# Linear attention into a Fourier mixing layer: even folds of the last two batches ahead of the odd ones, and the output stored through two disjoint views

## The chip, the cores and the metric

The kernel runs on one core of a Trainium2 chip. A core has a tensor engine (PE, whose weight loads are shown as PEld), a vector engine (DVE), a scalar engine (ACT), GpSimd (POOL) and a sync engine (SP) that issues transfers. Each engine takes its own instructions strictly in the order in which they were written for it, and engines wait for one another through semaphores. Transfers between the large memory (HBM) and the on-chip memory are started by SP, ACT or POOL. The metric is the device time of one execution in microseconds (us), lower is better. The time before is the median of three runs.

## The reference

Four batches of 768 positions go through two layers. The first is attention with a decay (8 heads of 64), in blocks of 64 positions, with a running state; its output becomes `x` of shape 4 x 768 x 512. The second is a Fourier mixing layer with a two-layer network:

```python
X = np.fft.fft(x, axis=1)
X = np.fft.fft(X, axis=2)
mixed = np.real(X)
u = x + mixed
un = (u - mean(u)) / np.sqrt(var(u) + 1e-06)
ch = np.maximum(un @ w_ch1, 0.0) @ w_ch2
return u + ch
```

`w_ch1` is 512 x 2048 and `w_ch2` is 2048 x 512. Everything is in 32-bit floats.

## The kernel before

**Stages.** The attention of a batch is computed in six chunks of 128 positions (`attn_in`, `attn_out`). The two-dimensional Fourier transform's real part is computed with cosine and sine matrices, after the input has been folded: positions and features that share a cosine (or, up to sign, a sine) are added or subtracted first, so that the matrices become smaller. Then come the normalization and the network. The network of the first four groups of rows (`PLAIN`, two row tiles of 128 each) is computed directly in `mlp`; the other eight groups (`LATE`) are put away in HBM and computed afterwards in four pairs with Strassen-like products, seven instead of eight (`first_layer`, `deep_first`, `deep_second`).

**Folds.** For each of a batch's two row blocks (`BLK`, 128 and 65 rows), `fold_a` makes the first half of the folds as soon as most of the attention is there, and `fold_b` the second half, when the last gathered rows have landed (the gather is an indirect transfer of POOL, line 461). `fold_b` goes through block 0 and then block 1. In each it makes an even operand `fe` (additions, lines 435, 438, 479, 480, 484, 485, with one small ACT copy on line 475) and an odd operand `fo` (subtractions, lines 436, 439, 488, 489, 492, 493). All of them run on DVE, and the built order alternates even and odd steps. Lines 435 and 436 are wide (512 elements per row), the others narrow (about 256).

**Products along the positions.** `fft_ln`, lines 520 to 530, makes five products `i` from these operands. Products 0, 1 and 4 read only `fe`, products 2 and 3 only `fo`. Each consists of four matmuls (line 525): two halves `n`, and in each block 0 and then block 1. An ACT copy (line 529) brings each result to the on-chip memory as `ys`, which the products of `width` (lines 537 to 542) read. The products are made in the order 0, 1, 2, 3, 4.

**What PE does beside it.** The folds of batches 2 and 3 are interleaved with the network of the plain groups: lines 643 (first layer), 649 and 651 (relu, on DVE and ACT in turn), 657 (second layer), 668 and 669 (DVE adds the residual to `y`). The interleaving is decided at build time from the amounts that the generators yield, so that a changed `yield` or a changed order of the folds also moves instructions of the network between them. The same holds for SP's queue.

**The end.** The last layer of the last pair is made by `deep_second(j, k)` for k = 0 to 6. Products k and k + 1 are interleaved: each consists of seven steps of four matmuls (`mm`, line 1047), and after each step `read` adds a quarter of the result on DVE (line 1055) or copies it on ACT (line 1053). `seven` fixes the order of the seven steps and which quarter each reads. The last product, k = 6, makes the second half of the columns of two row tiles, `yt[:, 0, 0]` and `yt[:, 0, 1]`. In the given order, the quarters of tile `yt[:, 0, 0]` end at steps 1 and 6, those of tile `yt[:, 0, 1]` at steps 4 and 5.

**Stores.** `store` (lines 628 to 634) writes a finished row tile. The first three row tiles of a batch lie in order and are stored by SP. The others are mirrored rows in reverse order, which an indirect store on POOL scatters row by row to the output. An indirect store gives the whole output as its destination, so the dependence tracking orders each direct store after the indirect stores recorded before it, and the other way round: SP waits until the rows have landed. At the end of a pair, `deep_second` issues four stores: after k = 5 the indirect one of `yt[:, 1, 1]`, after k = 6 the indirect one of `yt[:, 0, 1]` and the direct ones of `yt[:, 1, 0]` and `yt[:, 0, 0]`.

Of the kernel before, what the change touches and what calls it, by code (L numbers as in the profile page):

```python
# [9 lines left out]

# [6 lines left out]
ALU = mybir.AluOpType  # L17
# [59 lines left out]
def kernel(  # L77
# [10 lines left out]
    nc = tc.nc  # L88
    B, H, S, D = q.shape
    DM = H * D  # L90
# [3 lines left out]
    HC = NC // 2  # L94
# [4 lines left out]
    HM = DM // 2  # L99
    QM = DM // 4  # L100
    W = HM + 4
    BLK = [128, S // 4 + 1 - 128]
# [36 lines left out]
    def new(pool, shape, tag, **kw):  # L139
        cnt[0] += 1  # L140
        return pool.tile(shape, F32, tag=tag, name=f"{tag}{cnt[0]}", **kw)

    def psum_a(shape):
        return new(pa, shape, "pa")
# [40 lines left out]
    def row_of(j, n=128):  # L185
        return bass.IndirectOffsetOnAxis(ap=ix[0:n, j:j + 1], axis=0)
# [56 lines left out]
    xs, xn_, xd = {}, {}, {}  # L243
# [12 lines left out]
    ins, oTs, eo = {}, {}, {}  # L256
# [173 lines left out]
    def fold_x(b, a, n, i, lo, hi):  # L430

        e, o = eo[b][a]
        tt = nc.vector.tensor_tensor

        tc.keep_in_program_order(tt(e[0:n, i, 0:DM], lo, hi, op=ALU.add))
        tc.keep_in_program_order(tt(o[0:n, i, 0:DM], lo, hi, op=ALU.subtract))
        yield 1.4
        tt(e[0:n, i, 1:HM], e[0:n, i, 1:HM], e[0:n, i, HM:DM - 1], op=ALU.add)
        tt(o[0:n, i, 1:HM], o[0:n, i, 1:HM], o[0:n, i, HM:DM - 1], op=ALU.subtract)
        yield 0.8  # L440
# [24 lines left out]
    def fold_a(b):  # L465
        for a, n in enumerate(BLK):
            yield from fold_x(b, a, n, 1, eo[b][a][1][0:n, 1, 0:DM], xn_[b, HC + a][0:n])

    def fold_b(b, sets):

        tt = nc.vector.tensor_tensor
        for a, n in enumerate(BLK):
            yield from fold_x(b, a, n, 0, xs[b, a][0:n], xs[b, HC + a][0:n])
            e, o = eo[b][a]
            nc.scalar.copy(e[0:n, :, HM:HM + 1], e[0:n, :, DM - 1:DM])

            am, bm = e[0:n, :, W:2 * W], o[0:n, :, W:2 * W]
            lo, hi = e[0:n, 0, 0:HM + 1], e[0:n, 1, 0:HM + 1]
            tt(am[:, 0, 0:HM + 1], lo, hi, op=ALU.add)
            tt(am[:, 1, 0:HM + 1], lo, hi, op=ALU.subtract)  # L480
            yield 0.8

            lo, hi = am[:, :, 0:QM], am[:, :, HM:QM:-1]
            tt(e[0:n, :, 0:QM], lo, hi, op=ALU.add)
            tt(e[0:n, :, QM:HM], lo, hi, op=ALU.subtract)
            yield 0.8
            lo, hi = o[0:n, 0, 1:HM], o[0:n, 1, 1:HM]
            tt(bm[:, 0, 1:HM], lo, hi, op=ALU.subtract)
            tt(bm[:, 1, 1:HM], lo, hi, op=ALU.add)
            yield 0.8  # L490
            lo, hi = bm[:, :, 1:QM + 1], bm[:, :, HM - 1:QM - 1:-1]
            tt(o[0:n, :, 0:QM], lo, hi, op=ALU.subtract)
            tt(o[0:n, :, QM:HM], lo, hi, op=ALU.add)
            yield 0.8
            sets.append((e, o))
        eo.pop(b)
# [3 lines left out]
    def fft_ln(b):  # L500
        sets = []

        def piece(a, i, n):

            c0 = W + QM if i == 4 else QM * (i % 2)
            return sets[a][i in (2, 3)][0:BLK[a], n, c0:c0 + QM]

        if b in LEADS:
            yield from fold_a(b)
            yield from fold_b(b, sets)  # L510
            yield 2.0
        else:
            yield 1.0
            run(fold_a(b))
            yield 6.0 if b - 1 in LEADS else 3.0
            run(fold_b(b, sets))
            yield 12.0 if b - 1 in LEADS else 9.0


        for i in range(5):  # L520
            ps = psum_a([128, 2, NK])
            m = 128 if i < 4 else 1
            for n in range(2):
                for a, rows in enumerate(BLK):
                    mm = nc.tensor.matmul(ps[:, n, :], lhsT=piece(a, i, n), rhs=cs[0:rows, a, i in (2, 3), n, :],  # L525
                                          start=(a == 0), stop=(a == 1))
                    if i + n + a == 0:
                        tc.keep_in_program_order(mm)
            nc.scalar.copy(ys[i][0:m, 0:2 * NK].rearrange("p (k n) -> p n k", n=2), ps[0:m])
            yield 1.4  # L530
# [66 lines left out]
        for t in (1, 2, 0):  # L597
            ps = psum_a([128, DM])
# [13 lines left out]
            if t == 0:  # L612
                ps = psum_a([128, DM])
# [11 lines left out]
    ORDER = [(b, g) for b in range(B) for g in (1, 2, 0)]  # L625
    PLAIN, LATE = ORDER[:4], ORDER[4:]

    def store(b, T, y, cols=slice(0, DM)):
        if T < HC:
            nc.sync.dma_start(out[b, 128 * T:128 * T + 128, cols], y[:, cols])  # L630
        else:
            nc.gpsimd.indirect_dma_start(out=out.rearrange("b s d -> (b s) d"),  # L632
                                         out_offset=row_of(2 + HC * (b + 1) + T - HC),
                                         in_=y[:, :], in_offset=None)

# [75 lines left out]
    def quarters_a(t):  # L711

        return [t[:, s, i:i + HF // 2] for s in range(2) for i in (0, HF // 2)]

    def quarters_b(t):

        return [t[:, i:i + HF // 2, m:m + HM // 2] for i in (0, HF // 2) for m in (0, HM // 2)]
# [44 lines left out]
    def bank():  # L762
        return new(s2.ps, [128, DM], "p2")
# [12 lines left out]
    PAIRS = len(LATE) // 2  # L776
# [171 lines left out]
        for s in range(G):  # L948
            e.tensor_tensor(o[:, s], x[:, s], y[:, s], op=op)

    def seven(mm, read):

        X, Y, Z = (bank() for _ in range(3))
        for m, ps, start, where in ((0, X, True, (0, 0, 1)), (1, Y, True, (0, 0, 0)), (2, X, False, (1, 0, 1)),
                                    (3, Z, True, (1, 1, 1)), (4, X, False, (1, 1, 0)), (5, Z, False, (1, 0, 0)),
                                    (6, X, False, (0, 1, 1))):
            if m:
                yield 0.0
            mm(m, ps, start)
            read(ps, *where)  # L960
# [70 lines left out]
    def deep_second(j, k):  # L1031

        P = pairs[j]
        h, (a, b) = P.h, PRODUCTS[k]
        y11, y12, y21, y22 = P.y
        if k == 0:
            P.t = new(s2.yp, [128, G, HM], "t2")
        T = P.t
        y, fresh = ((T, 1), (y11, 1), (y22, 1), (T, 0), (y12, 1), (y21, 0), (y12, 0))[k]
        A11, A12, A3, A22 = [[t[:, i] for i in range(HF // 2)] for t in quarters_a(h[a])]  # L1040
        B11, T3, B21, B22 = quarters_b(s2.B[b])
        (S1, S2, S4), (T1, T2, T4) = P.pre_a.pop(k), P.pre_b.pop(k)
        ab = [(A11, B11), (A12, B21), (S2, T2), (A3, T3), (S1, T1), (A22, T4), (S4, B22)]

        def mm(m, ps, start):
            for i in range(HF // 2):
                nc.tensor.matmul(ps[:, 0:HM // 2], lhsT=ab[m][0][i], rhs=ab[m][1][:, i, :], start=(start and i == 0),  # L1047
                                 stop=(i == HF // 2 - 1), skip_group_check=True)

        def read(ps, s, m, first):  # L1050
            o = y[:, s, m * HM // 2:(m + 1) * HM // 2]
            if first and fresh:
                nc.scalar.copy(o, ps[:, 0:HM // 2])  # L1053
            else:
                V.tensor_tensor(o, ps[:, 0:HM // 2], o, op=ADD)  # L1055

        yield from seven(mm, read)

        def add_u(o, y, k, m):
            u = P.us[k][:, :, 0:HM] if m == 0 else P.us[k][:, :, DM - 1:HM - 1:-1]  # L1060
            nc.gpsimd.tensor_tensor(o, y, u, op=ADD)  # L1061

        who, yt = P.who, P.yt
        if k == 0:
            h["s2"] = h["a11"]
            if j < DEEP:
                split(h["s1"])
            part_sum(V, h["a11"], h["s1"], h["a11"], SUB)
        elif k == 1:
            V.tensor_tensor(y11, y11, T, op=ADD)  # L1070
            add_u(y11, y11, 0, 0)
        elif k == 2:
            if j < DEEP:
                split(h["a22"])
            h["s4"] = h["a12"]
            part_sum(V, h["a12"], h["a12"], h["s2"], SUB)
            if j == DEEP - 1:
                place_sums_w()
        elif k == 3:
            V.tensor_tensor(y22, y22, T, op=ADD)  # L1080
            add_u(y21, y22, 1, 0)
            add_u(T, T, 0, 1)
            add_u(y22, y22, 1, 1)
        elif k == 4:
            V.tensor_tensor(y22, y22, y12, op=ADD)
            V.tensor_tensor(y12, y12, T, op=ADD)
        elif k == 5:
            store(*who[1][1], yt[:, 1, 1])
        else:
            store(*who[0][1], yt[:, 0, 1])  # L1090
            store(*who[1][0], yt[:, 1, 0])
            store(*who[0][0], yt[:, 0, 0])

    def sum_s3(j):

# [94 lines left out]
    def run(gen):  # L1190
        return sum(gen)
# [82 lines left out]
```

## Time and profile before

| What | us |
|---|---|
| Median of three runs (from 790.59 to 792.36) | 791.47 |
| The profiled execution, its whole time | 791.45 |
| Its span, from the first to the last instruction | 789.2 |
| PE busy | 761.4 |
| DVE busy | 586.2 |
| DMA, mean share of the 16 engines between 240 and 270 us / 760 and 789.2 us | 0.20 / 0.28 |
| PE waiting for `fe` of line 484, both times together | 2.7 |
| SP waiting for indirect stores to land, six times together | 34.8 |

The span leaves out 2.25 us of the execution that lie around the first and last instruction. Busy times of engines overlap and don't add up to the span; a wait of an engine that isn't the bottleneck at that moment costs nothing. The idle time of PE is therefore what must be placed: where it lies, and what released PE at its end. In the profile a matmul of 32-bit floats appears as two records, so that "x8" in a row of line 525 or 657 stands for four matmuls.

### The profile page before, as it was taken

Reading aid. Unit: us, or ns where it says so; the run is one execution under the profiler, and the core shown is the slowest. Engines: PE = TensorE matmul, PEld = TensorE weight load, DVE = VectorE, ACT = ScalarE, POOL = GpSimd, SP = SyncE. Lnnn points to the kernel's source line nnn. Section 1 sums busy time; section 2 is a strip of 40 time slices with the busy share of each in tenths; the row PEclk is TensorE's granted clock in tenths of the full one; section 3 lists DMA queues with packets and bytes.
Section 4 is the critical chain, followed back from the end, with each engine's and each line's share of the span. In section 5 each row is a group of like instructions: output and inputs, shape, how many; then the busy total and the mean of one; then the engine's idle time right before and its main releaser. Section 6 shows DMA issues by size and latency. Waiting matters only on the chain.

```text
span 789.2 us, 14621 instructions
## 1 busy us (share of the span) xinstructions
PE 761.4 (96%) x5616; PEld 646.2 (82%) x5616; DVE 586.2 (74%) x1148; ACT 225.4 (29%) x532; POOL 198.2 (25%) x197
## 2 busy tenths in 40 slices
PE   6989989999999999999999999999999999999996
PEld 5767776858675877858846889988999999999996
DVE  5899889685846382345798998669966699758983
ACT  3765443325531221422101221022211342024300
POOL 3223331011102010211004950289105001220021
PEclk9999999999999999999999999999999999999998
DMA  9978723337843147521343375245944455455442
GB/s 230 266 157 226 197 100 121 93 65 208 224 134 87 54 81 146 135 87 41 72 102 107 149 253 151 89 174 200 350 144 148 148 176 185 130 172 186 127 124 79
DMA packets 152331, 116.80 MB, mean 148 GB/s; under 512 B 113998, under 2 KB 113998, under 8 KB 152262
## 3 DMA queue, kind: packets, MB, share of 16 engines
q1 hardware_dynamic: 147120, 103.39, 46.7%
q0 software_dynamic: 2112, 6.69, 2.5%
q10 hardware_dynamic: 3030, 5.78, 2.0%
q8 instruction: 45, 0.74, 0.4%
q14 instruction: 24, 0.20, 0.1%
HBM read 83.58 MB, written 32.25 MB: 147 GB/s over the span
## 4 chain that ended last, share of the span: by engine, by line
PE 82%; DVE 9%; DMA 4%; issue 2%; ACT 2%; POOL 1%; POOLq 0%; ACTq 0%
PE p L1047 22%; PE p L892 12%; PE p L977 11%; PE pm L657 11%; PE pm L643 10%; PE pa L525 3%; PE pa L341 3%; PE pa L300 3%; DMA x<-xb,ix 2%; PE pa L335 2%; PE pa L276 1%; PE pa L320 1%; PE pa L281 1%; PE pa L357 1%; DVE sc L304 1%
## 5 line engine op out<-in xcount | busy, mean ns | idle before, releaser
L643 PE MATMUL pm<-ut,w 128*128 128x256 f32 x512 | 118.4, 381 | 0.0
L657 PE MATMUL pm<-w,hr 128*128 128x512 f32 x256 | 115.3, 596 | 0.1
L643 PEld LDWEIGHTS pm<-ut,w 128*128 128x128 f32 x512 | 94.5, 190 | 13.6 <-issue 2.1
L657 PEld LDWEIGHTS pm<-w,hr 128*128 128x128 f32 x256 | 46.7, 190 | 50.3 <-issue 48.9
L1061 POOL TENSOR_TENSOR y<-y,u 128x512 f32<-128x512 f32 x12 | 18.9, 1571 | 199.1 <-DVE y L1070 156.7
L1047 PE MATMUL p<-tx,sx 128*128 128x128 f32 x416 | 54.9, 275 | 0.0
L1047 PEld LDWEIGHTS p<-tx,sx 128*128 128x128 f32 x416 | 50.6, 192 | 0.0
L892 PE MATMUL p<-ur,w 128*128 128x256 f32 x192 | 46.7, 379 | 0.0
L272 POOL TENSOR_TENSOR kd<-k,decay 128x512 f32<-128x512 f32 x20 | 22.6, 1129 | 95.4 <-PE pa L320 55.9
L1053 ACT COPY y<-p 128x128 f32<-128x128 f32 x48 | 12.8, 267 | 104.1 <-PE p L1047 103.1
L1055 DVE TENSOR_TENSOR y<-p,y 128x128 f32<-128x128 f32 x92 | 25.6, 286 | 22.5 <-PE p L1047 15.9
L892 PEld LDWEIGHTS p<-ur,w 128*128 128x128 f32 x192 | 36.4, 190 | 5.3 <-issue 0.5
L1047 PE MATMUL p<-w,ha 128*128 128x128 f32 x288 | 37.4, 275 | 0.0
L304 DVE TENSOR_TENSOR sc<-pa,decay 128x512 f32<-128x512 f32 x48 | 31.5, 683 | 7.4 <-PE pa L300 7.2
L300 PEld LDWEIGHTS pa<-qT,kT 64*128 64x128 f32 x384 | 26.1, 193 | 12.8 <-ACT qT L283 7.6
L1047 PEld LDWEIGHTS p<-w,ha 128*128 128x128 f32 x288 | 35.0, 192 | 0.2
L651 ACT ACTIVATE hr<-pm 128x256 f32<-128x256 f32 x44 | 16.7, 385 | 62.5 <-PE pm L643 62.2
L300 PE MATMUL pa<-qT,kT 64*128 64x128 f32 x384 | 30.8, 292 | 3.2 <-ACT qT L283 2.9
L892 PE MATMUL p<-sx,w1s 128*128 128x256 f32 x128 | 32.9, 380 | 0.5 <-DVE sx L795 0.5
L558 POOL TENSOR_SCALAR ve<-mv 128x2 f32<-128x2 f32 x12 | 3.3, 279 | 117.6 <-DVE mv L555 117.6
L341 PE MATMUL pa<-sc,v 128*64 128x128 f32 x384 | 30.6, 283 | 2.0 <-DVE sc L304 1.9
L632 POOL DMA_INDIRECT out_dram<-y,ix x12 | 12.7, 1057 | 77.3 <-DVE y L669 56.0
(234 smaller groups left out, 1734.7 us busy)
## 6 DMA issues: line engine op xcount, KB each, us to landing
tx<-td SPq DMA_DIRECT2D x84, 256.0 KB, 2.8
raw<-in_moe_w_ch_dram SPq DMA_DIRECT2D x32, 512.0 KB, 4.4
tx<-sd SPq DMA_DIRECT2D x42, 256.0 KB, 2.7
sd<-tx SPq DMA_DIRECT2D x28, 256.0 KB, 2.0
k<-in_k_dram SPq DMA_DIRECT2D x24, 256.0 KB, 5.9
q<-in_q_dram SPq DMA_DIRECT2D x24, 256.0 KB, 4.3
v<-in_v_dram SPq DMA_DIRECT2D x24, 256.0 KB, 5.1
td<-tx SPq DMA_DIRECT2D x21, 256.0 KB, 2.0
```

The lines of the kernel that those rows point to most:

```text
L272: nc.gpsimd.tensor_tensor(kd, kt, kpow, op=ALU.mult)
L300: mm(pss[hi][:, hp, :], lhsT=kT[HD[hi], hp, :], rhs=qT[HD[hi], hp, :], start=True, stop=True)
L304: nc.vector.tensor_tensor(t, pss[hi], decay[:, hi::2, :], op=ALU.mult)
L341: mm(po[HD[hi], hp, :], lhsT=vt[:, 2 * hp + hi, :], rhs=sc[hi][:, hp, :], start=(c == 0 and hp == 0), stop=(hp == HP - 1), skip_group_chec ...
L525: mm = nc.tensor.matmul(ps[:, n, :], lhsT=piece(a, i, n), rhs=cs[0:rows, a, i in (2, 3), n, :], start=(a == 0), stop=(a == 1))
L643: nc.tensor.matmul(ps, lhsT=w1[:, c, 128 * fc:128 * fc + 128], rhs=ut[:, c, :], start=(c == 0), stop=(c == KO - 1))
L657: nc.tensor.matmul(ps, lhsT=hr[(fc - f0) // 4][:, fc % 4, 128 * i:128 * i + 128], rhs=w2[:, fc, :], start=(fc == f0), stop=(fc == f1 - 1))
L892: nc.tensor.matmul(ps, lhsT=s2.A[a][:, kt, 128 * i:128 * i + 128], rhs=U[b][:, kt, :], start=(first and kt == 0), stop=(kt == 1), skip_gro ...
L977: nc.tensor.matmul(ps[:, 128 * i:128 * i + 128], lhsT=ab[m][0][:, 128 * i:128 * i + 128], rhs=ab[m][1], start=(start and i == 0), stop=Tru ...
L1047: nc.tensor.matmul(ps[:, 0:HM // 2], lhsT=ab[m][0][i], rhs=ab[m][1][:, i, :], start=(start and i == 0), stop=(i == HF // 2 - 1), skip_grou ...
L1055: V.tensor_tensor(o, ps[:, 0:HM // 2], o, op=ADD)
L1061: nc.gpsimd.tensor_tensor(o, y, u, op=ADD)
```

## The change

The change has four parts.

1. For batches 2 and 3 (`b > 1`), `folds_apart` takes the place of `fold_b`. It computes the same values with the same instructions, but makes the even operands of both blocks first, and then the odd operands of both.
2. For every batch, the five products are made in the order 0, 1, 4, 2, 3: those that read `fe`, then those that read `fo`.
3. The output is seen through two views that the dependence tracking treats as disjoint: direct stores go to `out_low`, indirect ones to `out_high`. Which rows are written is unchanged.
4. In the last pair, product k = 6 makes its steps in the order 0, 2, 3, 5, 4, 1, 6, and the stores are placed differently: the tile `yt[:, 1, 0]` and the first half of the columns of `yt[:, 0, 0]` are stored after k = 5, the second half of `yt[:, 0, 0]` in two quarters of the columns after k = 6.

```diff
+    def folds_apart(b, sets):
+
+        tt = nc.vector.tensor_tensor
+        parts = [(eo[b][a], xs[b, a][0:n], xs[b, HC + a][0:n], n) for a, n in enumerate(BLK)]
+        for (e, o), lo, hi, n in parts:
+            tc.keep_in_program_order(tt(e[0:n, 0, 0:DM], lo, hi, op=ALU.add))
+            tt(e[0:n, 0, 1:HM], e[0:n, 0, 1:HM], e[0:n, 0, HM:DM - 1], op=ALU.add)
+            nc.scalar.copy(e[0:n, :, HM:HM + 1], e[0:n, :, DM - 1:DM])
+            am = e[0:n, :, W:2 * W]
+            lo, hi = e[0:n, 0, 0:HM + 1], e[0:n, 1, 0:HM + 1]
+            tt(am[:, 0, 0:HM + 1], lo, hi, op=ALU.add)
+            tt(am[:, 1, 0:HM + 1], lo, hi, op=ALU.subtract)
+            lo, hi = am[:, :, 0:QM], am[:, :, HM:QM:-1]
+            tt(e[0:n, :, 0:QM], lo, hi, op=ALU.add)
+            tt(e[0:n, :, QM:HM], lo, hi, op=ALU.subtract)
+            yield 2.4
+        for (e, o), lo, hi, n in parts:
+            tc.keep_in_program_order(tt(o[0:n, 0, 0:DM], lo, hi, op=ALU.subtract))
+            tt(o[0:n, 0, 1:HM], o[0:n, 0, 1:HM], o[0:n, 0, HM:DM - 1], op=ALU.subtract)
...
+            tt(o[0:n, :, 0:QM], lo, hi, op=ALU.subtract)
+            tt(o[0:n, :, QM:HM], lo, hi, op=ALU.add)
+            yield 2.4
+            sets.append((e, o))
+        eo.pop(b)
...
-            run(fold_b(b, sets))
+            run((folds_apart if b > 1 else fold_b)(b, sets))
...
-        for i in range(5):
+        for i in (0, 1, 4, 2, 3):
...
+    out_low, out_high = dram_disjoint_views(out.rearrange("b s d -> (b s) d"), 2)
+
     def store(b, T, y, cols=slice(0, DM)):
         if T < HC:
-            nc.sync.dma_start(out[b, 128 * T:128 * T + 128, cols], y[:, cols])
+            row = S * b + 128 * T
+            nc.sync.dma_start(out_low[row:row + 128, cols], y[:, cols])
         else:
-            nc.gpsimd.indirect_dma_start(out=out.rearrange("b s d -> (b s) d"),
+            nc.gpsimd.indirect_dma_start(out=out_high,
...
-    def seven(mm, read):
+    def seven(mm, read, order=range(7)):
...
-        yield from seven(mm, read)
+        yield from seven(mm, read, (0, 2, 3, 5, 4, 1, 6) if (j, k) == (PAIRS - 1, 6) else range(7))
...
         elif k == 5:
             store(*who[1][1], yt[:, 1, 1])
+            if j == PAIRS - 1:
+                store(*who[1][0], yt[:, 1, 0])
+                store(*who[0][0], yt[:, 0, 0], slice(0, HM))
         else:
             store(*who[0][1], yt[:, 0, 1])
-            store(*who[1][0], yt[:, 1, 0])
-            store(*who[0][0], yt[:, 0, 0])
+            if j == PAIRS - 1:
+                for m in (0, HM // 2):
+                    store(*who[0][0], yt[:, 0, 0], slice(HM + m, HM + m + HM // 2))
+            else:
+                store(*who[1][0], yt[:, 1, 0])
+                store(*who[0][0], yt[:, 0, 0])
```

In the built programs every engine has the same arithmetic instructions before and after, in another order; SP has two more stores.

More of the change, by code (lines that the diff above doesn't have):

```diff
@@ L7 @@
 from concourse import mybir
+from concourse.bass_types import dram_disjoint_views
 from concourse.masks import make_identity
@@ L467, in fold_a @@
             yield from fold_x(b, a, n, 1, eo[b][a][1][0:n, 1, 0:DM], xn_[b, HC + a][0:n])
+    def folds_apart(b, sets):
[16 more added lines that the diff above has]
+            tt(o[0:n, 0, 1:HM], o[0:n, 0, 1:HM], o[0:n, 0, HM:DM - 1], op=ALU.subtract)
+            bm = o[0:n, :, W:2 * W]
+            lo, hi = o[0:n, 0, 1:HM], o[0:n, 1, 1:HM]
+            tt(bm[:, 0, 1:HM], lo, hi, op=ALU.subtract)
+            tt(bm[:, 1, 1:HM], lo, hi, op=ALU.add)
+            lo, hi = bm[:, :, 1:QM + 1], bm[:, :, HM - 1:QM - 1:-1]
+            tt(o[0:n, :, 0:QM], lo, hi, op=ALU.subtract)
[3 more added lines that the diff above has]
+        eo.pop(b)
     def fold_b(b, sets):
@@ L949, in part_sum @@
             e.tensor_tensor(o[:, s], x[:, s], y[:, s], op=op)
-    def seven(mm, read):
+    def seven(mm, read, order=range(7)):
         X, Y, Z = (bank() for _ in range(3))
-        for m, ps, start, where in ((0, X, True, (0, 0, 1)), (1, Y, True, (0, 0, 0)), (2, X, False, (1, 0, 1)),
-                                    (3, Z, True, (1, 1, 1)), (4, X, False, (1, 1, 0)), (5, Z, False, (1, 0, 0)),
-                                    (6, X, False, (0, 1, 1))):
+        steps = ((0, X, True, (0, 0, 1)), (1, Y, True, (0, 0, 0)), (2, X, False, (1, 0, 1)),
+                 (3, Z, True, (1, 1, 1)), (4, X, False, (1, 1, 0)), (5, Z, False, (1, 0, 0)),
+                 (6, X, False, (0, 1, 1)))
+        for m, ps, start, where in (steps[i] for i in order):
             if m:
```

## The prediction

> **What bounds the kernel now.** I read the page's busy totals first, then its chain, then busy time by stretches, and last the chain and timeline of each stretch in which TensorE (PE) stands idle.
>
> ```profile
> PE 761.4 (96%) x5616; PEld 646.2 (82%) x5616; DVE 586.2 (74%) x1148; ACT 225.4 (29%) x532; POOL 198.2 (25%) x197
> ...
> PE 82%; DVE 9%; DMA 4%; issue 2%; ACT 2%; POOL 1%; POOLq 0%; ACTq 0%
> ```
>
> PE is busy for 761.4 of 789.2 us, so only its 27.8 us of gaps can be won without taking work from it, and the change takes none. The stretches (columns: length, then busy us of PE, PEld, DVE, ACT, POOL) say where gaps lie near the edits:
>
> ```profile
> 240.00:270.00 30.00, 28.25 (x115) 19.52 (x114) 16.02 (x40) 5.91 (x16) 3.39 (x4) 1.00 0.20 62
> 270.00:350.00 80.00, 80.00 (x616) 58.95 (x615) 38.61 (x85) 20.49 (x51) 13.63 (x18) 1.00 0.49 114
> 350.00:380.00 30.00, 29.05 (x142) 24.32 (x141) 15.42 (x39) 5.88 (x17) 2.89 (x3) 1.00 0.11 36
> ...
> 424.00:760.00 336.00, 336.00 (x2600) 324.56 (x2599) 279.63 (x489) 77.32 (x187) 111.79 (x97) 1.00 0.53 171
> 760.00:789.20 29.20, 21.68 (x195) 21.49 (x193) 12.49 (x32) 1.07 (x4) 6.13 (x5) 0.93 0.28 90
> ```
>
> So 1.75 us are idle at batch 2's folds, 0.95 at batch 3's, 7.5 at the end, and none from 270 to 350 or 424 to 760. The chain of waits through batch 2's folds (start, length, what):
>
> ```profile
> 244.42 3.52 DMA x<-xb,ix
> ...
> 247.97 0.69 DVE fe L435
> 248.66 0.60 DVE fo L436
> ...
> 254.98 0.34 DVE fe L480
> 255.32 0.34 DVE fo L488
> 255.65 0.35 DVE fe L484
> 256.00 0.04 issue
> 256.04 2.08 PE pa L525 x11
> ```
>
> Even (fe) and odd (fo) steps alternate; PE's first product needs only even ones but waits for block 1's L484, behind nine odd steps. The end, from the timeline:
>
> ```profile
> 776.93 0.99 POOL L632 DMA_INDIRECT out_dram<-y,ix  x1 [5.50 <-DVE y L1055]
> ...
> 781.72 0.29 DVE L1055 TENSOR_TENSOR y<-p,y 128x128 f32<-128x128 f32 x1 [0.60 <-PE p L1047]
> 782.09 0.97 POOL L632 DMA_INDIRECT out_dram<-y,ix  x1 [4.16 <-DVE y L1055]
> 784.91 0.81 SPq L630 DMA_DIRECT2D out_dram<-y  x2
> ```
>
> Arithmetic ends at 782.01, yet SP's stores start at 784.91: SP's waits name the indirect stores (14.4 us, twice, longest 10.9).
>
> **What the Trainium skill says.** "Perfetto Trace Analysis", Optimizing Scalar/DVE Operations: where Vector isn't saturated but makes bubbles elsewhere, finer instructions may let work complete sooner; the 1.75 us beside a 74% busy DVE is such a bubble, here cured by order. "VectorE: DVE Perf Modes", The DRAIN you can't avoid: the next operation starts only after the pipe empties, and chained semaphores cost nothing extra. The trace disagrees: independent narrow folds start 0.34 apart though each takes 0.42, while L492, which reads L489's result, starts 0.45 after it. "DMA: Bandwidth & Descriptors", Anatomy of one DMA: about 2.0 us fixed, mostly completion; the indirect stores show 2.7 and 4.4. Same page, Issuing engines are not separate DMA queues: SP's and GpSimd's transfers share engines, so freed SP stores can slow the indirect ones.
>
> **Batch 2's folds.** No instruction is added or removed; order alone changes, and each fold now often follows the one it reads. Steps from the timeline: a wide fold followed by its reader 0.69 + 0.03 = 0.72; L438, ScalarE's copy L475, L479: 249.18 to 249.86 = 0.68; narrow independent 0.34, dependent 0.45. An even block is 0.72 + 0.68 + 0.34 + 0.45 + 0.34 + 0.34 = 2.87. From 247.97 block 1 starts at 250.84 and its L484 at 250.84 + 0.72 + 0.68 + 0.34 + 0.34 + 0.34 (the built order puts one residual add L668 there; its matmuls are over by 250.4) = 253.26, done 253.68. PE begins block 0's product at 253.81 and wants block 1 at 254.14. The whole 1.75 us wait goes. What is late next: the odd folds. Counting on likewise, block 1's first odd operand is done at 259.2; PE in its new order (8 even products of 0.33, four L657 products 3.44, the four products of i=4 1.31) asks for it after 261.2: 2.0 to spare. Bounds: 1.0, if the residual add stalls, to 1.8.
>
> **Batch 3's folds.** They start at 357.81, when gather DMA has landed. By the same steps, with two relus L649 in the even run (the first hides behind ScalarE's copy), block 1's L484 is done at 363.52. The new PE order puts only two L643 products before the first block 1 product, so PE arrives at 361.22 + 0.33 + 0.87 = 362.42 and waits 1.14 instead of 0.95: 0.19 lost. The odd operand is done at 368.8, wanted at 370.1. The relus' PSUM buffers are released no later than before. Bounds: a loss of 0.6 to a gain of 0.5.
>
> **Product order in batches 0 and 1.** The new order 0,1,4,2,3 applies there too, over unchanged folds. PE doesn't wait at these products (73.6 to 83 and 130.8 to 139.2), and ScalarE's last copy is the same 0.51 us for ys3 as for ys4: zero, hidden under PE's own queue; were the cover gone, one copy, 0.5.
>
> **Does the front's gain last?** From 266 everything that PE meets (loads of k, q, v, attention, batch 3's gather) is released by PE's own progress, so it shifts along. The one independent-looking stage, the weight sums on DVE (397 to 419.5), still waits 2.01 us for PE at 421.5, and its start follows PE as well.
>
> **The middle stores.** SP no longer waits for indirect landings at the end of pairs 0 to 2; the waits hid behind a full PE: zero. One store per pair and half of the last tile move ahead of some of SP's loads. The latter waits for GpSimd's add, over at 757.41; the load queued behind left at 757.59, will leave at about 757.8, and its data is used near 769. Zero; uncovered, 0.3.
>
> **The end.** The new interleaving of the last 14 groups of four products keeps PE's end at 781.69 and DVE's at 782.01. First indirect store: ready 776.65 as before, landing 781.32. The second still waits for that landing, although its data is now ready about 780.2; it starts 0.77 later, 782.09, lands at 784.8. SP's: one full tile from 778.4, a quarter row from 781.1, the last quarter from 782.05. Before, SP's pair left at 784.91, moved data from 785.7 to 787.4 and landed at 788.0: 0.8 before the data, 0.6 after. The last 64 KB: 782.1 + 0.8 + 0.5 + 0.6 = 784.0, ahead of the indirect store. GpSimd's own closing drain ran from 781.9 for 4.1 us, to 786.0; from the closing exchange's start, 788.5, to the span's end took 0.7. So the end comes at 786.0 + 0.7 = 786.7 on the old clock: 2.5 won. Bounds: 1.3, if SP's full tile delays the indirect stores by a microsecond, to 4.0: the first one's 4.4 us is its longest landing against a shortest of 2.7; at 2.7 SP's last part sets the end, 784.0 + 1.2 = 785.2.
>
> **Sum.** -1.75 + 0.19 - 2.5 = -4.06. The profiled execution took 791.45, of which the span is 789.2; it is 0.02 below the median of 791.47. 791.45 - 4.06 = 787.4.
>
> **Rivals.**
> - *The first indirect store also lands faster*: 4.0 at the end instead of 2.5, 785.9. For it: 2.7 is the commoner landing. Against: the cause of the 4.4 may sit at this place in every run.
> - *Only the end gains*: PE's lead is lost where something not paced by PE comes last, such as the weight sums or reloads before 424. For: PE already waits 0.5 there. Against: DVE's 2.01 us of slack. 791.45 - 2.5 = 789.0.
> - *The split doesn't do what it says*: the SP stores share engines with the indirect ones and delay them, so the end stays. For: the second indirect store still waits for the first. Against: moved data fills engines for only 1.7 us. 791.45 - 1.56 = 789.9.
> - *Slower, by dependent folds*: place, the even runs of batches 2 and 3. Each has three exposed dependent steps before PE's awaited product. If each costs x more than I took, the total is 6x - 0.41 (batch 2's slack) - 4.06; slower from x = 0.75 us, and 0.2% slower from 1.0. For: such steps were mostly interleaved away before. Against: L489 to L492, 0.45 in all. At x = 1.1: about 793.6.
>
> **How the numbers follow.** A change of 0.2%, 1.6 us, is about what measurement can tell from none. The forecast gets 0.68, the faster landing 0.09, only the end 0.09: faster 0.86. The third rival, at the bound, gets 0.08 as no change; slower 0.06. The forecast's own range is 786.3 to 788.6. The total range takes the good bounds in part (1.8, 0.5 and 4.0 would give 785.2) and the poor ones (1.0, -0.6, 1.3: 789.75): 785.6 to 789.8.
>
> **What will show it.** Right: no wait of PE for L484's successor near 254, about a microsecond of it near 362, PE still full to 424 and after; SP's last part store within 0.1 of DVE's last add; the last landing that of the indirect store. Wrong: PE waiting for odd operands, SP's direct stores landing last, a new PE gap between 266 and 424 as long as the one removed, or dependent folds over 0.5 apart.

## The result, and the profile after

The changed kernel takes 788.36 us (median of 22 runs, 786.85 to 792.22) against 791.07 us for the kernel before, measured beside it. The ratio is 0.9969, 95% interval 0.9957 to 0.9981, so about 2.5 us faster, and a second measurement on another occasion gave 0.9951 (0.9932 to 0.9969), about 3.9 us faster. Between the two occasions the median of the kernel before moved from 791.07 to 792.23 us, that of the changed kernel from 788.36 to 788.92. The forecast was 787.4 us, in a range of 785.6 to 789.8.

The profiled execution takes 787.12 us, and its span is 784.8 us instead of 789.2. Two lines of the page, busy time by engine and shares of the chain that ended last:

```profile
PE 759.8 (97%) x5616; PEld 645.4 (82%) x5616; DVE 588.4 (75%) x1148; ACT 225.1 (29%) x532; POOL 196.7 (25%) x197
...
PE 85%; DVE 8%; DMA 4%; ACT 2%; issue 1%; POOL 1%; POOLq 0%; ACTq 0%
```

PE does the same work and fills more of a shorter span. The stretches that were read before the change, after it (length, then busy us of PE, PEld, DVE, ACT, POOL; the granted clock, DMA share and GB/s are last):

```profile
240.00:270.00 30.00, 30.00 (x126) 21.36 (x125) 19.11 (x45) 6.03 (x17) 3.00 (x3) 1.00 0.21 69
270.00:350.00 80.00, 80.00 (x612) 57.97 (x611) 37.85 (x83) 20.87 (x53) 13.63 (x18) 1.00 0.48 110
350.00:380.00 30.00, 28.88 (x149) 25.40 (x148) 16.00 (x39) 5.86 (x18) 3.62 (x5) 1.00 0.16 53
424.00:760.00 336.00, 336.00 (x2611) 324.86 (x2610) 279.75 (x490) 77.25 (x187) 110.85 (x96) 1.00 0.53 171
760.00:784.80 24.80, 19.18 (x172) 18.99 (x171) 10.96 (x27) 0.80 (x3) 6.14 (x5) 0.95 0.31 92
```

PE has no idle time left from 240 to 270, has 1.12 us at batch 3's folds (0.95 before), and has 5.6 us at the end (7.5 before). Batch 2's folds no longer appear on the chain at all. Its pieces there, with start, length and what ran:

```profile
243.09 10.30 PE pm L691 x24
253.39 2.63 PE pa L556 x16
256.02 3.43 PE pm L691 x8
259.45 3.94 PE pa L556 x24
```

Line 556 is the former 525 and line 691 the former 657. PE goes from the network into the first two products and on without a gap. On DVE, the even folds start when the gathered rows have landed, and block 1's last one that PE needs ends at 252.71, before PE begins the first product:

```profile
246.99 0.69 DVE L475 TENSOR_TENSOR fe<-x,x 128x512 f32<-128x512 f32 x1 [2.48 <-DMA x<-xb,ix]
...
252.30 0.41 DVE L483 TENSOR_TENSOR fe<-fe 65x256 f32<-65x256 f32 x1
```

The last line of the chain above contains the odd products, and PE doesn't wait for them. The only wait for a fold that the list of waits still names (us in total, times, longest) is batch 3's:

```profile
PE pa L556 <- DVE fe L483: 1.1, 1, 1.1
```

The end, from the timeline (start, length, what, and in brackets the idle time before it and what ended it):

```profile
774.43 0.99 POOL L666 DMA_INDIRECT out_dram<-y,ix  x1 [5.49 <-DVE y L1090]
...
776.02 3.85 SPq L664 DMA_DIRECT2D out_dram<-y  x3
...
779.22 0.29 DVE L1090 TENSOR_TENSOR y<-p,y 128x128 f32<-128x128 f32 x1 [0.60 <-PE p L1082]
780.14 0.97 POOL L666 DMA_INDIRECT out_dram<-y,ix  x1 [4.72 <-DVE y L1090]
```

SP's three stores are issued from 776.02 to 779.87 and wait for no indirect store any more. The brackets of the last line name DVE, but DVE had long been done. The chain shows what the second indirect store waited for, the landing of the first:

```profile
774.43 4.95 DMA out_dram<-y,ix
779.38 0.02 issue
779.40 0.02 POOLq L666
779.42 0.50 issue
```

That landing took 4.95 us. It had been 4.39 before.

**Where the 4.3 us between the two profiled executions came from.** Both traces hold the same 5616 PE instructions, so the start of the one with the same number can be compared. Up to batch 2's folds the execution after is 0.51 us early (this arose in the first 60 us, where no edit is). Across batch 2's folds the lead grows by 2.08, across batch 3's it shrinks by 0.09, and from there it stays at 2.50 to the last matmul. From the last matmul to the span's end it is 7.54 us before and 5.66 after: 1.88 won. So the change accounts for 2.08 - 0.09 + 1.88 = 3.87 us, and the start for 0.51.

### The profile page after: what moved, and what is told of

Its sections match the earlier page's. It is cut to its first block, busy times and chain, and to the rows that moved or that the text cites. A ratio compares the mean times of both kernels' runs of the same rounds, so it can differ in the third digit from the quotient of the medians.

```text
span 784.8 us, 14617 instructions
## 1 busy us (share of the span) xinstructions
PE 759.8 (97%) x5616; PEld 645.4 (82%) x5616; DVE 588.4 (75%) x1148; ACT 225.1 (29%) x532; POOL 196.7 (25%) x197
## 4 chain that ended last, share of the span: by engine, by line
PE 85%; DVE 8%; DMA 4%; ACT 2%; issue 1%; POOL 1%; POOLq 0%; ACTq 0%
PE p L1082 22%; PE pm L691 12%; PE p L926 12%; PE p L1012 11%; PE pm L677 11%; PE pa L556 3%; PE pa L301 3%; PE pa L342 3%; PE pa L336 2%; DMA x<-xb,ix 2%; PE pa L321 1%; PE pa L277 1%; PE pa L358 1%; PE pa L282 1%; DVE sc L305 1%
```

## The experiments

All kernels compute the whole output. In the numbers below, the *front's shift* is how much PE's starts move across the folds, measured like that against the trace before (negative: earlier); the *tail* is the time from the last matmul's end to the end of the span. Edits are shown against the changed kernel.

### The two halves apart

**Front alone:** the old end, and one view of the output.

```diff
-        yield from seven(mm, read, (0, 2, 3, 5, 4, 1, 6) if (j, k) == (PAIRS - 1, 6) else range(7))
+        yield from seven(mm, read)
...
-    out_low, out_high = dram_disjoint_views(out.rearrange("b s d -> (b s) d"), 2)
+    out_low, out_high = [out.rearrange("b s d -> (b s) d")] * 2
```

(and the four stores back in their old places)

> Even folds first for batches 2 and 3 and the new product order, but the old end and one view of the output. Theory A (front and end are separate and add up): PE's instructions after batch 3's products start 2.0 us earlier than before (2.08 won at batch 2's folds, 0.09 lost at batch 3's), this lead stays to the last matmul, the time from the last matmul to the span's end stays 7.5 us, as before: time about -2.0 us. Rival B (only the end counts in the median): 0, between -0.5 and +0.5. Rival C (the new product order in batches 0 and 1 also moves something): the shift of PE's instructions at 140 us differs from that at 60 us by more than 0.2 us.

Measured: ratio 0.9974 (0.9955 to 0.9993), about 2.1 us faster. Shift across batch 2's folds -2.09, across batch 3's +0.15, constant afterwards. Theory A holds for the front, and B falls. Rival C's figure appears: the shift moves by 0.38 between 60 and 140 us. But 0.29 of it arises between 63.5 and 71.6, ahead of batch 0's first product, and a kernel with the old product order (the whole end, below) moves by 0.7 in that stretch, so it is no effect of the order. The tail wasn't the expected 7.5 but 8.3. The chain and the SP queue of this kernel show why:

```profile
773.99 4.93 DMA out_dram<-y,ix
```

```profile
782.51 1.01 SPq L664 DMA_DIRECT2D out_dram<-y  x2
```

The first indirect store takes 4.93 us though none of SP's output stores is under way then: they leave at 782.51. So the early SP store that my bound had named can't be what lengthens that landing here. The longer landing is 0.54 of the tail's 0.78; the rest is SP's pair, which now takes 4.55 us from its issue to the span's end instead of 4.31. So by its one trace the front alone is only 2.09 - 0.15 - 0.78 = 1.16 us faster; the ratio's interval, 0.6 to 3.6 us, takes in both figures.

**The views alone:** old folds, products, order of steps and places of the stores.

> The two disjoint views alone; folds, products, the order of the last product and the places of the stores are the old ones. Theory A (the views are what wins at the end, since GpSimd's closing drain comes last and both indirect stores stay where they were): SP's two full tiles leave at DVE's last add, 782.1 on the old clock, land near 785.2, and the end follows GpSimd's drain at 786.0 + 0.7: -2.5 us; -2.0 if the two tiles (0.5 MB) slow the second indirect store by half a microsecond. Theory D (the order of the last product and the stores in parts are needed too): SP's tiles and the second indirect store share the engines, the later of them lands near 787, and less than 1.0 us is won. In both the first indirect store lands after 4.4 us, as before.

Measured: ratio 0.9960 (0.9939 to 0.9980), about 3.2 us faster, and a tail of 4.76 us, 2.8 less than before and 0.9 less than in the whole change. Theory D falls. A is right on the direction and too low: like D it took the first landing as 4.4 us, and it was 3.00.

```profile
781.34 0.99 POOL L666 DMA_INDIRECT out_dram<-y,ix  x1 [5.50 <-DVE y L1090]
785.81 0.97 POOL L666 DMA_INDIRECT out_dram<-y,ix  x1 [3.48 <-DVE y L1090]
```

The second indirect store leaves 4.47 us after the first. Here DVE really is what it waited for: the chain gives the first landing as 3.00 us, at 784.35, and its data came 1.2 us later. SP's tile was not held back to DVE's end either: a first one left at 782.92, as soon as its own data was there.

**The whole end alone:** old folds and product order.

```diff
-            run((folds_apart if b > 1 else fold_b)(b, sets))
+            run(fold_b(b, sets))
...
-        for i in (0, 1, 4, 2, 3):
+        for i in range(5):
```

> The whole end (views, order of the last product, stores placed and in parts) over the old folds and product order. Theory A: the time from the last matmul to the span's end is 5.6 us, as in the changed kernel, instead of 7.5: -1.9 us. My first sum said -2.5. The first indirect store lands after 4.95 us if SP's full tile, which now leaves 1.6 us after it, is what delays it; after 4.4 if the 4.95 was an accident of one execution. Rival E (the end's gain is an effect of where the front puts it): 0.

Measured: ratio 0.9978 (0.9961 to 0.9994), about 1.7 us faster; tail 5.80 us; first landing 5.10 us. Theory A's size is met and E falls. The longer landing came again, so 4.95 was no accident of one execution; whether SP's tile is what delays it is looked at below. Together with the views alone this is an odd pair: adding the order of the steps and the parts to the views made the tail 1.0 us *longer*. The trace also gives a second sample of the old folds (PE at batch 2's products):

```profile
254.14 0.49 PE L556 MATMUL pa<-cs,fe 128*128 128x193 f32 x2
256.14 2.57 PE L556 MATMUL pa<-cs,fe 65*128 65x193 f32 x14 [1.51 <-DVE fe L515]
```

From block 0's first product to block 1's it is 2.00 us instead of the 0.33 that a product takes when nothing is missing: a stall of 1.67. In the trace before it was 256.04 - 253.81 - 0.33 = 1.90, from these lines, and in the kernel with one view, below, 1.53. From the first fold's start to PE's arrival at the product it is 6.08 us here, 5.84 in the trace before and 6.20 with one view; with the stall this makes 7.7 each time. So the old stall varies with the time between the landing of the gathered rows and PE's arrival.

```profile
253.81 0.49 PE L525 MATMUL pa<-cs,fe 128*128 128x193 f32 x2
256.04 2.57 PE L525 MATMUL pa<-cs,fe 65*128 65x193 f32 x14 [1.75 <-DVE fe L484]
```

**The whole change, beside them.**

> The changed kernel as it is, beside the parts. Theory A: the sum of the two halves, -2.0 - 1.9 = -3.9 us. Rival F (something holds the sum at the -2.4 to -2.7 us that the medians have shown): the front's and the end's parts, run alone beside it, add up to more than it by over 1 us.

Measured: ratio 0.9951 (0.9932 to 0.9969), about 3.9 us faster; shifts -2.08 and +0.04; tail 5.46. The halves give 2.1 + 1.7 = 3.8. The medians don't support rival F, but with intervals of 1.3 to 1.5 us each way for each half they can't exclude an excess of 1 us. In the traces the front's shift at batch 2 is the same alone and in the whole (-2.09 and -2.08), and the end gains 1.74 us alone and 1.88 and 2.08 in the two profiles of the whole; only the longer tail of the front alone, seen once, doesn't fit a plain sum.

### What in the end does the work

**Order and placed parts with one view:** the end without the views.

```diff
-    out_low, out_high = dram_disjoint_views(out.rearrange("b s d -> (b s) d"), 2)
+    out_low, out_high = [out.rearrange("b s d -> (b s) d")] * 2
```

(over the old folds and product order)

> The order of the last product and the placed stores in parts, over the old folds and product order, with one view of the output instead of two. Theory A (the views are the working part of the end): each direct store now waits for the indirect one recorded before it and the second indirect one for the direct ones: SP's full tile leaves at the first landing, about 4.9 us after the first indirect issue, lands about 2.9 later, only then the second indirect store leaves, and after its landing SP's last parts: the time from the last matmul to the end is 9 us or more instead of 7.5, so slower than before by 1 to 3 us. Theory D (the order and the parts do the work): faster than before by 1.5 us or more.

Measured: ratio 1.0025 (1.0007 to 1.0043), about 2.0 us slower; tail 10.15 us. The chain:

```profile
781.70 0.34 SPq L664
782.03 0.04 issue
782.08 2.01 DMA out_dram<-y
784.08 0.02 issue
784.11 0.04 POOLq L666
784.15 0.50 issue
```

Direct and indirect stores alternate, each waiting for the other kind to land. The second indirect store leaves only at 784.88, and SP's last parts after that. The views are what makes the end faster; the placement alone makes it slower.

**Views with the old order and places, under the new front.**

> The changed front and the two views, but the old order of the last product and the old places of the last stores (two full tiles after k = 6, no parts). Theory A (views do all of the end's work, since both indirect stores stay the same and GpSimd's drain comes last): as fast as the changed kernel, within 0.5 us, the time from the last matmul to the end 5.3 to 6.0. Rival G (the new order and the parts cost something: the early full tile of SP shares the engines with the instruction fetch, which took 1.7 to 1.9 us with it and 1.0 without): 0.5 to 1.0 faster than the changed kernel. Rival D (the parts are needed): SP's tiles land last, and 0.5 to 1.5 us slower than the changed kernel.

Measured: ratio 0.9943 (0.9927 to 0.9960), about 4.5 us faster; tail 4.76 us, again 0.7 to 0.9 less than the whole change. The two ratios can't be told apart, the tails can. Theory A's tail of 5.3 to 6.0 isn't met, and D falls.

```profile
776.69 0.99 POOL L666 DMA_INDIRECT out_dram<-y,ix  x1 [5.50 <-DVE y L1090]
...
778.27 3.87 SPq L664 DMA_DIRECT2D out_dram<-y  x2
...
781.15 0.97 POOL L666 DMA_INDIRECT out_dram<-y,ix  x1 [3.48 <-DVE y L1090]
```

Rival G has the right sign but its mechanism falls here: SP's tile leaves 1.58 us after the first indirect store, just as in the changed kernel (1.59), and yet that store lands after 3.04 us. And in the kernel with one view above, where SP stores nothing before 781.70, the first indirect store of 776.53 still takes 5.1 us. The packets of the transfers say more. In every kernel one fetch of 16 KB of instructions passes on one of the 16 DMA engines while the first indirect store is under way. The store's 256 KB go in 64 packets of 4 KB, four on each engine. Those that are behind the fetch come late. (The trace doesn't number the engines. That fetch and late packets share one is read from the times: each late packet begins as the piece before it ends, the first of them as the fetch ends, and at most four are late.)

```
                       first indirect store      instruction fetch   late packets
                       issue    packets          start    end        number  last end
before                 776.93   778.49-779.32    779.29   780.29     1       780.72
whole change           774.43   775.99-776.83    776.04   777.92     4       778.90
front and views        776.69   778.25-779.38    779.39   780.35     0
```

**Full tile last:** an attempt to move the tile away.

```diff
             if j == PAIRS - 1:
-                store(*who[1][0], yt[:, 1, 0])
                 store(*who[0][0], yt[:, 0, 0], slice(0, HM))
...
                 for m in (0, HM // 2):
                     store(*who[0][0], yt[:, 0, 0], slice(HM + m, HM + m + HM // 2))
+                store(*who[1][0], yt[:, 1, 0])
```

> The changed kernel, but SP's full tile of the last pair is stored last, after the two quarters, instead of ahead of the half. Theory G (that tile, which leaves 1.6 us after the first indirect store, slows the instruction fetch and so the first landing): the fetch takes 1.0 us instead of 1.7 to 1.9 and the first indirect store lands after 4.2 to 4.4 us instead of 4.95. Theory J (the fetch comes when it comes, and holds what lies behind it on its one engine): landing still 4.7 to 5.1. In both SP's last store now is a full tile at DVE's end, landing within 0.5 us of the second indirect store's landing, so the time from the last matmul to the end stays between 5.0 and 6.0.

Measured once: first landing 4.73 us, fetch from 776.96 to 778.63 (1.67 us), four packets behind it; tail 5.44.

```profile
775.35 4.73 DMA out_dram<-y,ix
```

This test failed to do what its text says. The planner that orders SP's queue put the tile's store where it had been: the built queue is the changed kernel's, and a store of 256 KB still left 1.59 us after the indirect one, at 776.94. So it is a repeat of the changed kernel, with the same delay, and tells G and J not apart; G's mechanism is refuted by the front with views and by the kernel with one view, not by this one.

**Old order of the steps, with the new places and parts.**

```diff
-        yield from seven(mm, read, (0, 2, 3, 5, 4, 1, 6) if (j, k) == (PAIRS - 1, 6) else range(7))
+        yield from seven(mm, read)
```

> The changed kernel with the last product's steps in the old order; views, places and parts of the stores as changed. It is to tell what holds the first indirect store: it landed after 3.0 us in both kernels with views and the old order and places, after 4.8 to 5.1 in all with the new order and places. Theory L (SP's two more instructions, or the places of its stores, bring the fetch forward): landing after 4.7 to 5.1 here too. Theory M (the order of the steps does): 3.0 to 3.1, no packet of that store behind the fetch, and the time from the last matmul to the end about 4.8.

Measured once: first landing 3.17 us, no packet behind the fetch, tail 4.54 us.

```profile
775.43 3.17 DMA out_dram<-y,ix
778.61 0.02 issue
```

Theory M, not L: the delay goes with the order of the steps. The edit also moved one of SP's two quarters ahead, to 774.29, 1.14 us before the indirect store; the tile left 1.59 us after it as in the changed kernel. The kernel with one view points the same way from the other side: new order, no store of SP near, four packets late. Over all profiles of this study:

| Kernel | Steps of the last product | Late packets of 64 | First landing, us | Last indirect store, after the last matmul's end | Tail, us |
|---|---|---|---|---|---|
| before | old | 1 | 4.39 | 0.40 | 7.54 |
| front alone | old | 2 | 4.93 | 0.94 | 8.32 |
| views alone | old | 0 | 3.00 | -0.29 | 4.76 |
| front and views | old | 0 | 3.04 | -0.29 | 4.76 |
| new parts, old order | old | 0 | 3.17 | -0.29 | 4.54 |
| three views, old end | old | 2 | 4.6 | -0.29 | 4.76 |
| whole change (two profiles) | new | 4, 4 | 4.95, 4.76 | 0.96, 0.77 | 5.66, 5.46 |
| whole end alone | new | 4 | 5.10 | 1.12 | 5.80 |
| tile late | new | 4 | 4.73 | 0.75 | 5.44 |
| old products | new | 4 | 4.03 | 0.04 | 5.63 |
| end with one view | new | 4 | 5.1 | 3.59 | 10.15 |
| three views | new | 4 | 5.0 | -1.18 | 3.67 |
| three views, batch 3 | new | 4 | 5.2 | -1.18 | 3.80 |

In all eight profiles with the new order, all four packets of that engine are behind the fetch; in the six with the old order none to two are. Why the order of the steps puts the fetch ahead of those packets stays open. It isn't simply that the fetch runs earlier: its record begins 2.6 and 2.8 us after the indirect store in the two last kernels of the table, with four late packets, and 2.7 after it in the three with none. In those two kernels the other 60 packets had ended 0.2 and 0.4 us before the fetch's record begins, and what held the four until then isn't in the trace.

In the kernels with views, the last two columns differ by 4.7 to 5.05 us (5.59 with the old products, where three packets of the *second* indirect store were behind another fetch). GpSimd's closing drain (the `DRAIN` that it runs at the program's end) ends 1.5 to 1.6 us after that store's last packet, and the span 0.8 after the drain. So the tail is when the last indirect store leaves, plus about 4.8 us.

**The last indirect store through a third view**, so that it need not wait for the first one's landing:

```diff
-    out_low, out_high = dram_disjoint_views(out.rearrange("b s d -> (b s) d"), 2)
+    out_low, out_high, out_last = dram_disjoint_views(out.rearrange("b s d -> (b s) d"), 3)
...
-            nc.gpsimd.indirect_dma_start(out=out_high,
+            nc.gpsimd.indirect_dma_start(out=out_last if (b, T) == (LATE[-2][0], TT[LATE[-2][1]][1]) else out_high,
```

> The changed kernel, but the last indirect store goes through a third disjoint view, so that it doesn't wait for the first one's landing. Theory A (the chain at the end runs through the first indirect landing, held up behind an instruction fetch): the last indirect store leaves 0.3 us after its last DVE add, 1.5 to 2.2 us before the end of DVE instead of 0.6 after it; what comes last is then either indirect landing or SP's last part, and the time from the last matmul to the end is 3.5 to 4.5 instead of 5.6: -4.9 to -6.0 us against before. Rival H (GpSimd issues or moves the two one after the other anyway, or the closing drain takes its 4.1 us whenever it starts): no gain over the changed kernel, -3.9.

Measured: ratio 0.9916 (0.9883 to 0.9949; 7 runs), 786.25 us against 792.61, about 6.7 us faster than before; tail 3.67 us, 2.0 less than the changed kernel.

```profile
774.42 0.99 POOL L666 DMA_INDIRECT out_dram<-y,ix  x1 [5.49 <-DVE y L1090]
...
778.00 0.97 POOL L666 DMA_INDIRECT out_dram<-y,ix  x1 [2.58 <-DVE y L1090]
...
779.22 0.29 DVE L1090 TENSOR_TENSOR y<-p,y 128x128 f32<-128x128 f32 x1 [0.60 <-PE p L1082]
```

The store leaves at 778.00, 0.28 after its last add (777.43 to 777.72), ahead of DVE's end. The first landing still took 5.0 us, with four late packets, but nothing waits for it now. Theory A holds, H falls. This version beats the kernel before by its interval; over the changed kernel the intervals overlap a little (0.9883 to 0.9949, and 0.9932 to 0.9969 for the changed one on its own occasion), and it is the traces, with the same front and a tail 2.0 us shorter, that put it ahead. They account for 2.07 + 3.87 = 5.9 us against before; the rest of the 6.7 isn't placed, and there are only seven runs.

**Three views with the old order and places.**

> The changed front and three views, with the old order of the last product and the old places of the last stores. Theory A (with the second indirect store free of the first's landing, the order of the steps and the parts begin to count, because DVE's end plus a transfer now comes last): the last indirect store leaves 0.9 us later than with the new order, SP's last full tile at DVE's end; the time from the last matmul to the end is 4.2 to 4.8, against 3.7 with the new order and parts: -4.5 us against before. Rival D2 (the order and the parts are worth nothing there either): 3.5 to 3.8.

Measured: ratio 0.9954 (0.9926 to 0.9983; 9 runs); tail 4.76 us.

```profile
779.10 0.97 POOL L666 DMA_INDIRECT out_dram<-y,ix  x1 [3.48 <-DVE y L1090]
```

The store leaves 0.29 us before the last matmul's end, 0.9 later than with the new order, as theory A said. The tail is that of two views with the old order, since there too this store waited for DVE and not for the landing. So the new order, with the places and parts that came with it, earns its 0.9 us at this store (1.1 us of tail) only with the third view. With two views it is paid for: its data is ready earlier, but the store waits for a landing that has become later.

### The front in detail

**Old product order, with the folds apart.**

```diff
-        for i in (0, 1, 4, 2, 3):
+        for i in range(5):
```

> The changed kernel with the five products in the old order 0, 1, 2, 3, 4. Theory A (the new product order gives nothing of its own: in batch 2 PE asks for the first odd operand at 259.3 and the last one at 259.6, and they are done at 255.9 and 258.5): PE's lead over the kernel before grows by the same 2.1 us across batch 2's folds, and changes across batch 3's by less than 0.4 us. Rival K (the order is needed): PE waits for an odd operand, more than 0.5 us in either batch.

Measured once: shifts -2.09 across batch 2's folds and +0.13 across batch 3's, as with the new order. The one wait for a fold is still this:

```profile
PE pa L556 <- DVE fe L483: 1.1, 1, 1.1
```

Theory A: the product order is worth nothing of its own, because with the folds apart the odd operands are ready before PE asks even in the old order. The single time, 788.96 us, isn't comparable within a microsecond.

**More network work ahead of batch 3's products** (over the three views):

```diff
-            yield 12.0 if b - 1 in LEADS else 9.0
+            yield 12.0 if b - 1 in LEADS or b == 3 else 9.0
```

> The kernel with three views, and in batch 3 the planner is told a larger amount between the folds and the products (12 instead of 9), which puts two more groups of four first-layer matmuls (1.74 us) ahead of the first product. Theory A (PE's wait of 1.1 us at batch 3's products is only a matter of what work stands there): the wait goes, and PE's lead after batch 3 is 3.0 to 3.2 us instead of 2.0; 1.1 us faster than the kernel with three views alone, if nothing later asks for the products' results earlier. Rival I (the work moved ahead is missing later, behind the products or at the start of the late layers): PE waits for ys or for the sums there, gain below 0.3 us.

Measured: ratio 0.9926 (0.9902 to 0.9949; 9 runs), not to be told from the three views alone. In the trace, PE at batch 3's products has no wait left:

```profile
351.67 10.52 PE L677 MATMUL pm<-ut,w 128*128 128x256 f32 x48
362.03 2.79 PE L556 MATMUL pa<-cs,fe 128*128 128x193 f32 x16
```

The lead grows by 1.30 us across these folds, but 0.73 of it is lost again between 384 and 414 us, where PE meets a new wait:

```profile
PE pm L691 <- DVE hr L683: 0.5, 1, 0.5
```

A net 0.57 us stays, between the two theories: the work moved ahead is missing in part when the second layer is short of relus.

## Why the prediction was right

**Batch 2's folds, -1.75: right, and larger.** I took the idle time that the profile put down to this wait. The stall itself was 1.90 us by the starts of the matmuls, since the first product's modelled end reaches over part of it; the shift against the trace before was 2.08. The other 0.18 lies in two small steps, 0.07 ahead of the product and 0.10 behind it, that nothing here explains. Other samples of the old folds stalled 1.67 and 1.53, so the edit is worth 1.5 to 2.1 us, depending on which old execution it is held against. The even operand of block 1 was done 5.72 us after the first fold's start (246.99 to 252.71), where my steps gave 5.71 (247.97 to 253.68). A dependent step took 0.44 to 0.46 us, or 0.71 to 0.73 for a wide fold and its reader. The rival of slow dependent folds falls with that: its x was about zero.

**Batch 3's folds, +0.19: right.** PE waited 1.12 us, where I had said 1.14; the shift was +0.09, and -0.05 to +0.18 in the other kernels, but for the one with more work put ahead of batch 3's products.

**Product order and middle stores, 0: right.** Nothing shifts at batches 0 and 1 that can be put down to the order, the old order gave the same shifts at batches 2 and 3, and PE's lead is constant to 0.02 us from 440 us to the last matmul.

**The front's lead lasts: right.** PE is full from 270 to 350 and from 424 to 760. That also disposes of the rival in which only the end gains.

**The end, -2.5: the mechanism right, the size too large by 0.6.** The failed step is "First indirect store: ready 776.65 as before, landing 781.32", which took over the landing of 4.39 us unchanged. It measured 4.95, 0.56 more, and everything behind it (the second store 0.77 later, GpSimd's drain, the closing exchange) came as I had it, 0.6 later. My bound named SP's full tile as what might delay it. The runs showed an instruction fetch with the store's packets on its engine behind it, and that the step order, which I had costed as moving no engine's end, goes with the delay. The rival of the faster landing didn't come true in the changed kernel. Where no packet was late the landing did take 3.0 to 3.2 us, but only with the old order, in which the second store then waits for its data, and the end gained 2.8 to 3.0 us, not the 4.0 that the rival said. Of the signs of being right, SP's last part left 0.03 us after DVE's last add (779.51 to 779.54), and none of the signs of being wrong appeared. The rival in which SP's stores keep the end where it was falls with the views alone.

**The sum.** -2.08 + 0.09 - 1.88 = -3.87 in the traces, against my -4.06: the front's surplus (0.43) and the end's shortfall (0.62) nearly cancelled, so that the sum comes out this close is in part luck. The repeated ratio, -3.9, agrees. The first one, -2.5, is lower, and -4.06 lies outside its interval of -3.4 to -1.5; whether the difference is more than scatter between occasions stays open.

## What to carry to other kernels

A dependence that tracking sees and the data doesn't have is worth finding first: the two disjoint views alone shortened the end by 2.8 us, more than the whole change did (1.9), and one more view on the last store took another 2.0 us off the changed kernel's end. The new order with the finer split of the stores lost 2.0 us without the views, and cost 0.7 to 1.0 us with two. Once such a wait is gone, ask what the freed instruction waits for next, here the landing of a transfer whose length isn't fixed; an edit that makes data ready earlier earns nothing until that wait is gone too. Making what is consumed first also first in the queue of a busy engine removed a stall without touching any work; what it is worth is best read from starts of the consumer's instructions, not from the idle time beside modelled ends.

## What the runs showed of the hardware

**Instruction fetches share the DMA engines.** A fetch of 16 KB took 0.96 to 1.9 us on one engine, and up to four of the 64 packets of an indirect store, all that fell to this engine by its even share, waited behind it. Of the 128 packets of SP's tile in the changed kernel, 120 moved between 776.86 and 777.69, and 8 only from 778.90, as the last late packet of the indirect store ended. The landing went from 3.0 to as much as 5.2 us, with the same amount of data. The Trainium skill's "DMA: Bandwidth & Descriptors", Issuing engines are not separate DMA queues, says that transfers of different issuers share the engines; these traces agree, and count the fetches among them.

**An indirect store spends most of its fixed time ahead of its data.** The second one before was issued at 782.09, moved its packets from 783.63 to 784.47 and landed at 784.83: 1.54 us ahead of the data and 0.36 behind it. The prediction quotes "mostly completion" for the fixed part; for this store the measurement says otherwise.

**The closing drain of GpSimd follows the last indirect store's packets.** It lasted 4.1 to 4.5 us in nearly all profiles (5.0 where a second fetch came between), and ended 1.5 to 1.6 us after the last packet.

**The granted clock drops now and then for a few microseconds.** In the profiled execution of the views alone, the clock was at half for 6.8 us from 69.1 and for 3.4 us from 260.2. In the busy time by stretches of that kernel, the third number from the right is the mean granted clock, 0.83 and 0.86, where the kernel before has 1.00 in the first:

```profile
62.00:82.00 20.00, 17.78 (x179) 15.84 (x180) 17.48 (x34) 8.85 (x21) 5.67 (x4) 0.83 0.89 237
258.00:270.00 12.00, 11.30 (x46) 8.84 (x46) 3.40 (x10) 2.02 (x4) 1.01 (x1) 0.86 0.12 44
```

PE's instructions were 2.45 us later across the first of these. The profiles of the old product order and of the front with views have one such drop each, 3.4 us from 70.1 and 70.2. An episode costs as much as the whole effect measured here, and the scatter of one kernel's runs goes with the clock: of the 75 runs of the kernel before on the second occasion, the 21 with a mean granted clock of 0.998 or more have a median of 791.0 us, the 17 with 0.994 or less one of 796.5. That is why the traces' shifts and tails carried the argument and not single times.
